# One row of the last weight matrix loaded in three unequal parts

## The chip, the cores and the metric

The kernel runs on one core of a Trainium2 chip. The metric is the device time of one execution in microseconds (us). Before the change it is 401.03 us, the median of three runs (400.92 to 401.08).

## The reference

One token (a row of 1,024 numbers, bf16) goes through two blocks side by side, and their outputs are added to it.

```python
xn = _layernorm(x)
return x + _A_ref(xn, A_k_cache, A_v_cache, A_wq, A_wo) + _B_ref(xn, B_w1, B_w2, B_w3, B_w4)

# A: attention of 32 query heads over 4 cached key/value heads of 65,536 positions, 128 wide
q = (x @ wq) as 32 heads
p = softmax(q k^T * 128 ** -0.5);  o = p v;  A = o @ wo

# B: a mixer and an MLP. For one token the shifted quarters of h are all zero,
# so the first matrix product adds nothing:
x1 = x + shifted(gelu(layernorm(x) @ w1)) @ w2
B = x1 + gelu(layernorm(x1) @ w3) @ w4
```

The weights and the caches are 170 MB, each byte of which is used once. w4 has 3,584 rows of 1,024 numbers, 7.3 MB.

## The kernel before

The kernel keeps one stream of loads going through three slots of 64 KB a partition (`big`, `SLOTS = 3`). The stream, in order, is wq, w3, w1 with w2, then for each of eight units of 32,768 keys a K tile and a V tile of 8 MB, with wo between the last K and the last V, and w4 at the end. `Stream.pump` issues the next load, on SP's queue, as soon as `done` says that a slot is free, so at most three loads are under way or in use. Every load spreads over all 128 partitions; the sixteen DMA engines take eight partitions each.

For a K tile (`compute_k`, L345) the vector engine transposes the tile in place (L357), TensorE multiplies it with the queries (L362), and the maximum, the exponential and one more transpose (L367 to L383) give the weights. For a V tile (`compute_v`, L402) TensorE multiplies the weights with the values (L412), four matmuls side by side at four places of the array, 32 columns each.

Everything that is added to the output row is gathered in one PSUM bank, `psB`. The 1,024 outputs are kept as two halves of 512: the half j lies in row 32 * j, and `row_acc(j, lhsT, rhs)` (L220) adds one product to it. TensorE writes half 0 from the array's columns from 0 on and half 1 from those from 32 on (`tile_position`), and the two matmuls of a pair can be under way together. Its callers are the start with x itself and its layer norm (L281), w2 (L340), the projection of the last head group (L449), the sum of the projections of the others (L459) and w4 (L465). In the kernel before, `row_acc` repeats the single column of weights 32 times, so that rows 0 to 31 all hold half 0 and rows 32 to 63 all hold half 1.

The end of the kernel is this. After the last K tile the slot that it held goes to w4, whose load (L179 to L184) is cut into eight pieces along the 28 rows that each partition holds: 6, 5, 6, 4, 3, 2, 1 and 1 rows (`W4_PIECES`). A row here is 1,024 numbers, 2,048 bytes, in each of the 128 partitions. The wo projections of three head groups run (L451), then the last V tile. Then come the first 11 rows of w4 (`compute_w4`, L461), the projection of the last group through `row_acc`, and the other 17 rows as their pieces land: for each row a pair of matmuls, one for each half. ScalarE casts `psB[0:64]` to bf16 (L485), and a load queue of its own stores two rows of it, 31 and 32, which lie next to each other and hold one half each (L486).

Two passes over the finished program matter here. `keep_loaded_weights` drops a weight load where the same weights stand at the same place of the array already. `close_on_the_store` makes the end of the program wait for the store alone.

Of the kernel before, what the change touches and what calls it, by code (L numbers as in the profile page):

```python
# [17 lines left out]
SUBS = 4  # L18
SETS = 4
SLOTS = 3  # L20
W4_PIECES = (6, 5, 6, 4, 3, 2, 1, 1)


def keep_loaded_weights(nc):
# [68 lines left out]
def kernel(  # L93
# [14 lines left out]
    nc = tc.nc  # L108
# [3 lines left out]
    D = A_x.shape[-1]  # L112
# [9 lines left out]
    assert DH == P and HQ // HKV == 8 and HKV == 4 and D == 1024 and F == 3584 and S == 1  # L122
    assert SK % UKEYS == 0 and sum(W4_PIECES) == FC
    NB = SK // UKEYS
# [22 lines left out]
    class Stream:  # L147
# [17 lines left out]
        def load(self, it):  # L165
            t = big.tile([P, ROW], BF16, name="big")
            self.tiles[it] = t
            go = nc.sync.dma_start
            if it == "wq":
                go(out=t[:], in_=A_wq.rearrange("(p c) n -> p (c n)", c=DC))  # L170
            elif it == "w3":
                go(out=t[:, 0:DC * F], in_=B_w3.rearrange("(p c) f -> p (c f)", c=DC))
            elif it == "w12":
                go(out=t[:, 0:DC * D], in_=B_w1.rearrange("(p c) n -> p (c n)", c=DC))
                go(out=t[:, DC * D:2 * DC * D], in_=B_w2.rearrange("(m c) n -> m (c n)", c=DC))
            elif it == "wo":
                go(out=t[:].rearrange("p (g n) -> p g n", g=HKV),
                   in_=A_wo.rearrange("(g p j) n -> p g (j n)", g=HKV, p=P))
            elif it == "w4":  # L179
                w4_v = B_w4.rearrange("(m c) n -> m c n", c=FC)  # L180
                c0 = 0
                for n in W4_PIECES:
                    go(out=t[:, c0 * D:(c0 + n) * D], in_=w4_v[:, c0:c0 + n, :].rearrange("p c n -> p (c n)"))
                    c0 += n  # L184
            else:
                kind, i = it
                g, b = divmod(i, NB)
                cache = A_k_cache if kind == "K" else A_v_cache
                go(out=t[:], in_=cache[0, g, b * UKEYS:(b + 1) * UKEYS, :].rearrange("(p ct) d -> p (ct d)", p=P))
# [8 lines left out]
    ident_f = const.tile([P, P], F32, name="ident_f")  # L198
# [9 lines left out]
    for b in range(2):  # L208
        nc.gpsimd.tensor_copy(
            out=spread[:, 2 * b:2 * b + 2, :].rearrange("p r (a i) -> p r a i", a=4),  # L210
            in_=ident_f[:, 64 * b:64 * b + 64].rearrange("p (i r) -> p r i", r=2).unsqueeze(2).to_broadcast([P, 2, 4, 32]))
# [6 lines left out]
    psB = ps_B.tile([P, 512], F32, name="psB")  # L218

    def row_acc(j, lhsT, rhs, start=False):  # L220
        nc.tensor.matmul(psB[32 * j:32 * j + 32, :], lhsT=lhsT.to_broadcast([lhsT.shape[0], 32]), rhs=rhs, start=start,  # L221
                         stop=False, tile_position=(0, 32 * j), skip_group_check=True)

    x_t = ppool.tile([P, DC, 32], BF16, name="x_t", tag="p")
    for a in range(4):
        nc.vector.transpose(out=x_t[32 * a:32 * a + 32].rearrange("p c j -> p (c j)"),  # L226
                            in_=x_row[:, 256 * a:256 * (a + 1)].rearrange("p (i c) -> p c i", c=DC))
# [3 lines left out]
    def layernorm(src, tag):  # L231
# [39 lines left out]
                          in_=sel8[:].unsqueeze(2).to_broadcast([P, 8, 16]))  # L271
# [5 lines left out]
    accx = ppool.tile([1, D], F32, name="accx", tag="p")  # L277
    nc.vector.tensor_scalar(out=accx[:], in0=x_row[0:1, :], scalar1=ln_s1[0:1, 0:1], scalar2=ln_s2[0:1, 0:1],
                            op0=ALU.mult, op1=ALU.add)
    for j in range(2):  # L280
        row_acc(j, ident_f[0:1, 0:1], accx[0:1, 512 * j:512 * (j + 1)], start=True)  # L281

    def row_matmul(acc, rep, cols, widths):
        for c in range(DC):
# [44 lines left out]
    def compute_w12():  # L329
        wt = st.tiles["w12"][:, 0:2 * DC * D].rearrange("p (w c n) -> p w c n", w=2, c=DC)  # L330
        ps1 = ps_S.tile([P, SUBS, 512], F32, name="ps1", tag="sc")
        for c in range(DC):
            for q in range(2):
                nc.tensor.matmul(ps1[0:32, q, :], lhsT=xn2_rep[:, c, :], rhs=wt[:, 0, c, 512 * q:512 * (q + 1)],  # L334
                                 start=(c == 0), stop=(c == DC - 1), tile_position=(0, 0))
        h1 = ppool.tile([32, 2, 512], BF16, name="h1", tag="p")
        nc.scalar.activation(out=h1[:], in_=ps1[0:32, 0:2, :], func=ACTF.Gelu_apprx_tanh)
        for c in range(DC):
            for j in range(2):
                row_acc(j, g_col[:], wt[:, 1, c, 512 * j:512 * (j + 1)])  # L340
        st.done("w12")
# [60 lines left out]
    def compute_v(u):  # L402
        g, b = divmod(u, NB)
        if b == 1:
            og, wb, ol = group_weights()
        vt = st.tiles[("V", u)][:].rearrange("p (s u t d) -> p s u t d", u=SUBS, s=SETS, t=16)
        oacc = ps_O.tile([P, 512], F32, name="oacc")
        pT = group["p"]
        for e in range(SUBS):
            for t in range(16):  # L410
                q = t % 4
                nc.tensor.matmul(oacc[32 * q:32 * (q + 1), :], lhsT=pT[:, e, 32 * t:32 * (t + 1)],  # L412
                                 rhs=vt[:, :, e, t, :], start=(e == 0 and t < 4),
                                 stop=(e == SUBS - 1 and t >= 12), tile_position=(0, 32 * q))
        st.done(("V", u))
        if b == 0:
            og = ogpool.tile([P, 512], F32, name="og", tag="og")
            nc.scalar.copy(out=og[:], in_=oacc[:])
            group["og"] = og
            return  # L420
        nc.vector.scalar_tensor_tensor(out=og[:], in0=oacc[:], scalar=wb[:, 1:2], in1=og[:],  # L421
                                       op0=ALU.mult, op1=ALU.add)
        group_rows(g, og, ol)
# [20 lines left out]
    def project(g):  # L444
        wt = st.tiles["wo"][:].rearrange("p (g j n) -> p g j n", g=HKV, j=8)
        for j in range(8):
            for h2 in range(2):
                if g == HKV - 1:
                    row_acc(h2, oT[g][:, j:j + 1], wt[:, g, j, 512 * h2:512 * (h2 + 1)])  # L449
                    continue  # L450
                nc.tensor.matmul(tail["rows"][0:1, h2, :], lhsT=oT[g][:, j:j + 1],  # L451
                                 rhs=wt[:, g, j, 512 * h2:512 * (h2 + 1)], start=(g == 0 and j == 0),
                                 stop=(g == HKV - 2 and j == 7), tile_position=(0, 0))
# [7 lines left out]
    def compute_w4(lo, hi):  # L461
        wt = st.tiles["w4"]
        for c in range(lo, hi):
            for j in range(2):
                row_acc(j, hT[:, c:c + 1], wt[:, D * c + 512 * j:D * c + 512 * (j + 1)])  # L465
# [9 lines left out]
    for g in range(HKV - 1):  # L475
        project(g)
    add_projection()
    compute_v(NU - 1)
    early = sum(W4_PIECES[:2])
    compute_w4(0, early)  # L480
# [3 lines left out]
    out_t = ogpool.tile([64, 512], BF16, name="out_t", tag="og")  # L484
    nc.scalar.copy(out=out_t[:], in_=psB[0:64, :])  # L485
    nc.scalar.dma_start(out=out[0, 0, :].rearrange("(j n) -> j n", j=2),  # L486
                        in_=out_t[31:33, :])

# [1 line left out]
_INS = ['A_x', 'A_k_cache', 'A_v_cache', 'A_wq', 'A_wo', 'B_x', 'B_w1', 'B_w2', 'B_w3', 'B_w4']  # L490
# [26 lines left out]
```

## Time and profile before

| what | before |
|---|---|
| median of three runs | 401.03 us |
| the profiled execution, its own time | 400.92 us |
| its span, first to last instruction | 398.9 us |
| mean granted TensorE clock | 0.803 |
| share of the span that the load queue's packets fill, of 16 engines | 98.9% |
| busy: TensorE, weight loads, VectorE, ScalarE, GpSimd | 58%, 11%, 52%, 7%, 1% |
| read from HBM | 169.87 MB, 426 GB/s |

The page gives the busy time of each engine (PE is TensorE's matmuls, PEld its weight loads, DVE VectorE, ACT ScalarE, POOL GpSimd, SP the engine that issues the loads), and the span in 40 equal slices with the busy share in tenths. Where a line of the page reads `out<-in`, it names what is written and what is read; the number after L is a line of the kernel. The chain of work that ended last is followed back from the last instruction, at each step to what released it.

Beside the pages, the trace keeps for each load the moments at which its engines reported that their part had landed, sixteen for a load on all engines, and the start, size and duration of every packet. It does not name the engine of a packet.

### The profile page before, as it was taken

To read this page: it belongs to the slowest core of one execution; us is meant where nothing else is said; L and a number is where in the kernel's file an instruction comes from. 1 tells how busy PE (TensorE), PEld (TensorE's weight loads), DVE (VectorE), ACT (ScalarE), POOL (GpSimd) and SP (SyncE) were. 2 spreads that over 40 slices of the span, in tenths; PEclk is the share of its full clock that TensorE was granted. 3 is DMA by queue.
4 is the path that set the end of the run, shared out by engine and by line. 5 is a ranking of instruction groups with operands and counts; after the bars stand their busy time and mean duration, and the time that the engine had idled before them with its cause. 6 is when DMAs were issued, how large, how long until landed. Compare 5 with 4: busy or idle time off the path is not lost.

```text
span 398.9 us, 2547 instructions
## 1 busy us (share of the span) xinstructions
PE 232.8 (58%) x1348; PEld 45.1 (11%) x854; DVE 209.0 (52%) x154; ACT 27.3 (7%) x35; POOL 5.3 (1%) x28
## 2 busy tenths in 40 slices
PE   0571970591479238742974196539462945494987
PEld 0210000010100110010101010200020101010133
DVE  0601010964196569634953895269439942884130
ACT  1001010003000200020002000200100011002000
POOL 2000000000000000000000000000000000000000
PEclk9995996596869687956795889569855997698889
DMA  9998999999999999999999999999999999999996
GB/s 421 421 454 369 440 447 486 421 427 421 416 435 421 427 493 416 427 427 427 435 421 421 486 421 427 422 427 434 434 422 460 434 427 389 424 457 447 390 418 258
DMA packets 4575, 170.01 MB, mean 426 GB/s; under 512 B 467, under 2 KB 469, under 8 KB 982
## 3 DMA queue, kind: packets, MB, share of 16 engines
q1 hardware_dynamic: 4560, 169.87, 98.9%
q8 instruction: 8, 0.13, 0.1%
q14 instruction: 1, 0.01, 0.0%
q10 hardware_dynamic: 6, 0.00, 0.0%
HBM read 169.87 MB, written 0.00 MB: 426 GB/s over the span
## 4 chain that ended last, share of the span: by engine, by line
DMA 58%; DVE 20%; PE 18%; ACT 2%; issue 1%; DVEq 0%; ACTq 0%
DMA big<-in_A_k_cache_dram 34%; DVE big L357 14%; DMA big<-in_B_w_dram 14%; DMA big<-in_A_v_cache_dram 11%; PE sc L362 7%; PE oacc L412 5%; PE psh L287 3%; DVE p_sb L383 2%; DVE mx L367 2%; ACT p_sb L380 2%; PE ps L334 1%; PE psB L221 1%; PE pm_mx L369 0%; DVE m L371 0%; DVE ol L432 0%
## 5 line engine op out<-in xcount | busy, mean ns | idle before, releaser
L362 PE MATMUL sc<-big,qdiag 128*128 128x512 bf16 x512 | 128.5, 411 | 66.3 <-DVE big L357 66.1
L357 DVE STREAM_TRANSPOSE big<-big 128x4096 f32<-128x4096 f32 x32 | 139.4, 4413 | 50.1 <-DMA big<-in_A_k_cache_dram 50.1
L412 PE MATMUL oacc<-big,p_sb 128*32 128x512 bf16 x512 | 43.9, 511 | 34.5 <-DVE p_sb L383 34.5
L367 DVE TENSOR_REDUCE mx<-sc 128x1 f32<-128x2048 f32 x8 | 18.3, 2292 | 29.8 <-PE sc L362 29.8
L362 PEld LDWEIGHTS <-qdiag 128*128 128x128 bf16 x128 | 13.1, 103 | 177.1 <-issue 145.1
L380 ACT ACTIVATE p_sb<-sc,nball 128x2048 bf16<-128x2048 f32 x8 | 15.7, 1967 | 219.8 <-DVE nball L378 219.8
L383 DVE STREAM_TRANSPOSE p_sb<-p_sb 128x2048 bf16<-128x2048 bf16 x8 | 18.5, 2311 | 18.0 <-ACT p_sb L380 18.0
L412 PEld LDWEIGHTS <-p_sb 128*32 128x32 bf16 x512 | 16.5, 124 | 58.6 <-DVE p_sb L383 35.1
L287 PE MATMUL psh<-big,ln_rep_b 128*32 128x512 bf16 (+1 forms) x64 | 12.8, 968 | 7.5 <-DMA big<-in_B_w_dram 7.5
L451 PE MATMUL o_acc<-big,oT 128*1 128x512 bf16 x48 | 13.0, 440 | 2.4 <-ACT p_sb L380 2.4
L369 PE MATMUL pm_mx<-ident_f,mx 128*1 128x128 f32 x8 | 2.4, 295 | 19.1 <-DVE mx L367 19.1
L326 DVE STREAM_TRANSPOSE h_row<-h_row 128x896 bf16<-128x896 bf16 x1 | 1.1, 1112 | 21.0 <-ACT h_row L325 21.0
L421 DVE SCALAR_TENSOR_TENSOR og<-oacc,wb,og 128x512 f32<-128x512 f32 x4 | 3.0, 746 | 15.7 <-PE oacc L412 15.7
L221 PE MATMUL psB<-big,hT 128*32 128x512 bf16 x56 | 8.3, 430 | 0.3 <-DMA big<-in_B_w_dram 0.3
L457 DVE COPY o_rows<-o_acc 1x1024 f32<-1x1024 f32 x1 | 1.2, 1212 | 13.8 <-PE oacc L412 13.8
L235 PE MATMUL pm_ln<-ln_rowsum_a,ones_f 128*128 128x1 f32 x2 | 0.6, 347 | 12.6 <-DVE ln_rowsum_a L233 12.6
L433 PE MATMUL pm_e<-ol,sel8big 128*128 128x129 f32 x8 | 2.6, 414 | 7.9 <-DVE ol L432 7.9
L287 PE MATMUL psq<-big,ln_rep_a 128*32 128x512 bf16 x64 | 6.4, 585 | 1.3 <-DMA big<-in_A_wq_dram 1.3
L311 POOL COPY qdiag<-qx 32x32 bf16<-32x32 bf16 x16 | 3.2, 203 | 279.1 <-PE sc L362 249.1
L226 DVE STREAM_TRANSPOSE x_t<-x_row 32x256 bf16<-32x256 bf16 x4 | 2.5, 616 | 8.2 <-DMA x_row<-in_A_x_dram 8.1
L299 DVE CAST q_row<-psq 128x512 bf16<-128x512 f32 x1 | 0.7, 692 | 8.4 <-PE psq L287 8.4
L376 PE MATMUL pm_mx<-ident_f,rep 1*128 1x1 f32 x8 | 1.9, 240 | 5.0 <-DVE rep L373 5.0
(95 smaller groups left out, 73.6 us busy)
## 6 DMA issues: line engine op xcount, KB each, us to landing
big<-in_A_wo_dram SPq DMA_DIRECT2D x1, 8192.0 KB, 35.9
big<-in_B_w_dram SPq DMA_DIRECT2D x1, 7168.0 KB, 38.2
big<-in_B_w_dram SPq DMA_DIRECT2D x2, 2048.0 KB, 46.0
big<-in_B_w_dram SPq DMA_DIRECT2D x2, 1536.0 KB, 27.2
big<-in_B_w_dram SPq DMA_DIRECT2D x1, 1280.0 KB, 23.9
big<-in_B_w_dram SPq DMA_DIRECT2D x1, 1024.0 KB
big<-in_B_w_dram SPq DMA_DIRECT2D x1, 768.0 KB, 30.6
big<-in_B_w_dram SPq DMA_DIRECT2D x1, 512.0 KB, 31.4
```

What stands on the lines that cost most here:

```text
L221: nc.tensor.matmul(psB[32 * j:32 * j + 32, :], lhsT=lhsT.to_broadcast([lhsT.shape[0], 32]), rhs=rhs, start=start, stop=False, tile_positio ...
L287: nc.tensor.matmul(acc[32 * q:32 * q + 32, i, 0:n], lhsT=rep[:, c, :], rhs=cols(c, i, q), start=(c == 0), stop=(c == DC - 1), tile_positio ...
L311: nc.gpsimd.tensor_copy(out=qdiag[at, LEAD:].rearrange("p (x c) -> p x c", x=4)[:, :, 32 * a:32 * a + 8], in_=qx[at, :, 8 * g:8 * g + 8])
L334: nc.tensor.matmul(ps1[0:32, q, :], lhsT=xn2_rep[:, c, :], rhs=wt[:, 0, c, 512 * q:512 * (q + 1)], start=(c == 0), stop=(c == DC - 1), til ...
L357: nc.vector.transpose(out=words, in_=words)
L362: nc.tensor.matmul(sc[:, e, :], lhsT=qdiag[:, c0:c0 + P], rhs=cols[:, s, e, :, b2, :, r], start=(s == 0 and b2 == 0 and r == 0), stop=(s = ...
L367: nc.vector.reduce_max(out=mx[:], in_=sc[:].rearrange("p e n -> p (e n)"), axis=AX.X)
L380: nc.scalar.activation(out=p_sb[:], in_=sc[:], func=ACTF.Exp, bias=nball[:, b:b + 1], scale=SCALE, accum_out=group["lall"][:, b:b + 1])
L383: nc.vector.transpose(out=flat, in_=flat)
L412: nc.tensor.matmul(oacc[32 * q:32 * (q + 1), :], lhsT=pT[:, e, 32 * t:32 * (t + 1)], rhs=vt[:, :, e, t, :], start=(e == 0 and t < 4), stop ...
L421: nc.vector.scalar_tensor_tensor(out=og[:], in0=oacc[:], scalar=wb[:, 1:2], in1=og[:], op0=ALU.mult, op1=ALU.add)
L451: nc.tensor.matmul(tail["rows"][0:1, h2, :], lhsT=oT[g][:, j:j + 1], rhs=wt[:, g, j, 512 * h2:512 * (h2 + 1)], start=(g == 0 and j == 0), ...
```

## The change

Two things change.

The piece of 4 rows of w4 becomes one of 3 rows and one of 1. That one row is loaded by three DMAs, of the first 85 partitions, the next 30 and the last 13. A DMA's partitions are shared out evenly over as many engines as divide them: 85 go to the lowest 5 engines, 17 each, 30 to the lowest 15, 2 each, and 13 to the lowest 13, 1 each. So engines 0 to 4 carry 20 partitions of this row, 5 to 12 carry 3, 13 and 14 carry 2, and 15 carries none, where each carried 8.

The repeating of the weights goes: `row_acc` loads the single column that it is given and writes one row of `psB`. Only the first call keeps 32 columns, of which 31 are zero, so that all of `psB[0:64]` is written once. The store takes rows 0 and 32.

```diff
-W4_PIECES = (6, 5, 6, 4, 3, 2, 1, 1)
+W4_PIECES = (6, 5, 6, 3, 1, 3, 2, 1, 1)
+W4_SHARED = 4
+SHARES = (85, 30, 13)
...
-                for n in W4_PIECES:
+                for i, n in enumerate(W4_PIECES):
+                    if i == W4_SHARED:
+                        p0 = 0
+                        for k in SHARES:
+                            go(out=t[p0:p0 + k, c0 * D:(c0 + n) * D],
+                               in_=w4_v[p0:p0 + k, c0:c0 + n, :].rearrange("p c n -> p (c n)"))
+                            p0 += k
+                        c0 += n
+                        continue
...
     def row_acc(j, lhsT, rhs, start=False):
-        nc.tensor.matmul(psB[32 * j:32 * j + 32, :], lhsT=lhsT.to_broadcast([lhsT.shape[0], 32]), rhs=rhs, start=start,
-                         stop=False, tile_position=(0, 32 * j), skip_group_check=True)
+        nc.tensor.matmul(psB[32 * j:32 * j + lhsT.shape[1], :], lhsT=lhsT, rhs=rhs, start=start, stop=False,
+                         tile_position=(0, 32 * j), skip_group_check=True)
...
-        row_acc(j, ident_f[0:1, 0:1], accx[0:1, 512 * j:512 * (j + 1)], start=True)
+        row_acc(j, ident_f[0:1, 0:32], accx[0:1, 512 * j:512 * (j + 1)], start=True)
...
     nc.scalar.dma_start(out=out[0, 0, :].rearrange("(j n) -> j n", j=2),
-                        in_=out_t[31:33, :])
+                        in_=out_t[:].rearrange("(a b) n -> a b n", b=32)[:, 0, :])
```

## The prediction

> **What bounds the kernel now.** I read the page first, then the chain in order of time, then the DMA share in narrow stretches at the end, then the timeline of the same stretch.
>
> ```profile
> span 398.9 us, 2547 instructions
> PE 232.8 (58%) x1348; PEld 45.1 (11%) x854; DVE 209.0 (52%) x154; ACT 27.3 (7%) x35; POOL 5.3 (1%) x28
> DMA  9998999999999999999999999999999999999996
> q1 hardware_dynamic: 4560, 169.87, 98.9%
> q8 instruction: 8, 0.13, 0.1%
> ```
>
> All sixteen DMA engines are busy from start to end (98.9% in the one load queue), and no compute engine passes 58%. The loads set the time, so only what happens when they run out can move it. The chain in order of time ends so:
>
> ```profile
> 337.13 41.98 DMA big<-in_A_v_cache_dram
> 379.11 0.02 issue
> 379.12 17.39 DMA big<-in_B_w_dram
> 396.52 0.04 issue
> 396.56 0.41 PE psB L221 x2
> 396.97 0.02 issue
> 396.99 0.58 ACT out_t L485
> ```
>
> The last piece of w4 lands at 396.52, one pair of matmuls, the cast and the store follow, and the span ends at 398.9. This execution took 400.92, 0.11 under the median of 401.03; 2.0 us of it lie around the span, and I leave them and everything after 396.52 as they are. The columns below are the stretch, its length, each engine's busy time, the clock, the DMA share and GB/s.
>
> ```profile
> 394.20:394.40 0.20, 0.20 (x6) 0.10 (x2) 0.00 (x0) 0.00 (x0) 0.00 (x0) 1.00 1.06 410
> 394.60:394.80 0.20, 0.20 (x6) 0.08 (x4) 0.00 (x0) 0.00 (x0) 0.00 (x0) 1.00 0.52 195
> 395.20:395.40 0.20, 0.20 (x4) 0.11 (x3) 0.00 (x0) 0.00 (x0) 0.00 (x0) 1.00 0.58 215
> 395.60:395.80 0.20, 0.20 (x4) 0.00 (x0) 0.00 (x0) 0.00 (x0) 0.00 (x0) 1.00 0.52 195
> 396.00:396.20 0.20, 0.20 (x2) 0.02 (x2) 0.00 (x0) 0.00 (x0) 0.00 (x0) 1.00 0.01 0
> ```
>
> The share does not fall at once: it stands between 0.5 and 0.7 for 1.4 us. Some engines have run out while about half still load. The trace's landing events of the last piece say which times: six engines report at 394.77 to 395.02, one at 395.43, one at 395.81, eight at 396.21 to 396.52. The same events tell why: after the first load only one engine stood apart (0.88 us; the others lay within 0.47), and each of the eight packets of 16 KB in the queue named instruction moves one engine back by some 1.5 us (the one at 383.06: from 0.19 to 1.73 behind the first). It stays back for good, since every load gives each engine the same eight rows. The mean of the sixteen landings is 395.75: levelling them perfectly would win 0.77 us, 0.19%. I count 0.2% (0.8 us) as what a measurement here can tell from no change, so faster by more is all but shut out.
>
> **The shared row, if rows cost what they cost now.** The price of a row (2,048 bytes into one partition) stands in the timeline, in the starts of the last two pairs:
>
> ```profile
> 395.92 0.10 PEld L221 LDWEIGHTS <-hT 128*32 128x32 bf16 x2 [0.32 <-issue]
> 396.56 0.39 PE L221 MATMUL psB<-big,hT 128*32 128x512 bf16 x2 [0.25 <-DMA big<-in_B_w_dram]
> ```
>
> They are 0.64 us apart, one piece of eight rows an engine: 0.08 us a row. In the change engines 0 to 4 take 17 + 2 + 1 = 20 rows of the shared row, 5 to 12 take 3, 13 and 14 take 2, 15 none, where each took 8. So the lowest five get 12 more (0.96 us), the rest 5 to 8 fewer (0.40 to 0.64). If those five are among the six early ones, they end at 395.73 to 395.98, and the latest of the late at 396.52 - 0.40 = 396.12: the end comes 0.40 us earlier.
>
> **What rows cost when they are crossed.** Until now an engine always wrote its own eight rows of each load. Now 20 rows of each low engine fall into partitions that other engines are filling in the same microseconds with the pieces around it. The trace shows no such meeting, so I bound it. Below: nothing, 0.08 us a row; a gain per row is excluded, since an engine alone already runs at this pace. Above: the one row where foreign bytes meet an engine's stream is the instruction packet, which put an engine back 1.54 us for 16 KB, while a 16 KB packet of its own takes 0.61 us (eight of them end 4.9 us apart, 43.04 to 47.94): 2.5 times the bytes' time, 0.20 us a row. Two streams that simply alternate lie between, 0.16. I take 0.16, for it is the nearer to the only row with a meeting, without that row's fetch delays. Then a low engine needs 20 x 0.16 = 3.20 us instead of 0.64, 2.56 more, and its last landing moves from 395.02 to 397.58, 1.06 past today's end. At 0.20 it is 3.36 more, 398.38, +1.86. The late engines, with 3 rows at 0.16 (0.48) instead of 0.64, and 8 rows of others pressed into their partitions (8 x 0.08), end at 396.52 + 0.48 = 397.00, and do not decide. The break-even price is (396.52 - 395.02 + 0.64) / 20 = 0.107 us a row, and it is slower by 0.8 us from 0.147.
>
> [...]
>
> **Issues and waits.** Eleven loads are issued for w4 instead of eight; an issue takes SP 0.33 to 0.43 us, so 1.3 us more.
>
> ```profile
> 361.56 17.89 SPq L183 DMA_DIRECT2D big<-in_B_w_dram  x8
> ```
>
> This takes 17.9 us because the eighth waits, 14.4 us, for the V load that used the same landing counter (379.11). Eight counters go round, so the eighth of the new list (three rows) waits there too, and numbers nine to eleven (2, 1 and 1 rows) wait for the first three pieces, which landed at 382.81, 385.88 and 389.58. Nothing else is queued behind them on SP but the end's own waits. The last is issued at about 389.6 + 0.4; the store's packets ran 0.75 us after its issue began, and the earliest engine reaches that piece at 394.1: 3 us of cover, cost nothing. Without it each microsecond of lateness would be one of span. The pair for the shared row waits for three loads instead of one; checks of a passed semaphore took SP 0.02 to 0.03 us. The low engines come to that row at 389.6 to 389.9 (the landings of the old four-row piece, 390.25 to 390.52, less eight rows) and end it 3.2 us later, at 393.1; PE, which is behind its loads there, comes to it at 394.29. So 1.2 us of cover; beyond that each microsecond would hold back the seven pairs behind it.
>
> **Weights of one column, and the store.** row_acc now loads one column instead of 32 copies. The loads of 32 took 97 ns (median of 56, L221), those of one column 84 (24 in the projection, L451): 13 ns each, beside matmuls that start in pairs every 0.216 us. On the path lies at most the last one: -0.01 us. Against it: L451's one-column matmuls, all in one column group, go one after another, 0.43 us for two. L221's go two at once because j = 0 and 1 stand at columns 0 and 32; those places are kept, so I count nothing (the other end is a rival). The cast still reads 64 x 512 (0.58 us). The store takes rows 0 and 32 instead of 31 and 32: two packets of 1 KB, 47 and 46 ns side by side; from nothing to 0.05 us, I take nothing.
>
> Sum: +1.06 - 0.01 on this execution (401.97), and on the median 401.03 + 1.05 = 402.1.
>
> **The rivals.** *Free crossing* (0.30): a row costs 0.08 us wherever it goes; the end is levelled, -0.40 us, 400.6. For it: the engines' pace is the same for packets of 2 and 64 KB, which reads like an engine's own limit. Against: it supposes spare room on the writing side that 98.9% busy engines never showed. This is the case on the other side; it decides below 0.107 us a row. *A late engine among the low five* (0.13): no view names the engines; if one of the eight late ones is numbered 0 to 4, its 0.96 us come on top of 396.52: 402.0 even with free crossing. For it: eight of sixteen are late. Against: the one-partition load of x fits into the stream of an engine that more likely ends early, by the packets' times, which leave two or three candidates. *Both* (0.10): 396.52 + 2.56, 403.6. *Pairs lost* (0.03): if one-column matmuls ran singly, the 25 pairs after 390.41 would take 10.8 us at 0.43 and end at 401.2, not 396.97: +4.2, 405.3. Against: the column places.
>
> **How the numbers follow.** Crossing paid, low five early: 0.40, at 402.1, own range 401.5 to 402.9, of which 0.04 lies within 0.8 us of before. Free crossing 0.30, all within it. A late engine 0.13, 0.02 of it within. Both 0.10 and pairs lost 0.03, slower. What is left, 0.04, is a gain near full levelling or beyond, faster. Slower: 0.36 + 0.11 + 0.10 + 0.03 = 0.60; same 0.36; faster 0.04. The range reaches from 400.5 (free crossing, with 0.1 for the store and spread) to 403.1 (0.20 a row, and 0.2 over), and leaves out both and pairs lost, 0.13, and half of the faster cases.
>
> **What would show it.** Crossing is right if packets of the shared row take well over 84 ns and the last landings spread wider than 1.75 us, with few engines at the very end; the DMA share would then end in a long low step. Free crossing shows as a drop from 1.0 to near 0 within 0.7 us and a last landing near 396.1. A late low engine shows as one to three landings a microsecond behind the rest, packets at 84 ns. Lost pairs show as L221 pairs 0.43 us apart with no DMA wait. The prediction is wrong above all if writing into a neighbour's partitions is free.

## The result and the profile after

The changed kernel takes 403.27 us (median of six runs, 403.03 to 403.55) against 401.10 before (six runs as well): 2.17 us more, a ratio of 1.0055 with a 95% interval of 1.0042 to 1.0068. A second set of runs of the same kernel, below, gave 403.01 against 401.14. The profiled execution took 403.40 us.

The page of the kernel after, its first lines:

```profile
span 401.3 us, 2551 instructions
PE 233.7 (58%) x1348; PEld 44.6 (11%) x854; DVE 209.0 (52%) x154; ACT 27.3 (7%) x35; POOL 5.3 (1%) x28
GB/s 418 418 446 385 457 470 431 418 418 425 420 471 438 431 425 413 438 425 470 433 418 425 425 431 438 459 431 418 425 439 425 438 451 382 425 462 438 392 391 186
q1 hardware_dynamic: 4721, 169.87, 98.7%
q8 instruction: 8, 0.13, 0.1%
```

The load queue is as full as before (98.7%), the engines' busy times are nearly the same, and the same bytes are moved. The span is 2.4 us longer, and the last slices of the GB/s row are where it went. The chain in order of time ends so:

```profile
379.49 16.24 DMA big<-in_B_w_dram
395.73 0.04 issue
395.77 3.17 PE psB L231 x14
398.94 0.02 issue
398.96 0.58 ACT out_t L495
```

The end has moved from 396.99, where the cast began, to 398.96, and the path now goes through seven pairs of matmuls instead of one: in this execution the clock granted to them was 0.50, and they stood about 0.42 us apart. The landing events put the last landing of w4 at 398.28, against 396.52; the last pair starts 0.04 us behind it in both profiles. In narrow stretches of the kernel after (columns as in the prediction: the last three are clock, DMA share, GB/s):

```profile
389.00:390.00 1.00, 1.00 (x14) 0.39 (x10) 0.09 (x1) 0.00 (x0) 0.00 (x0) 1.00 1.01 338
390.00:391.00 1.00, 1.00 (x12) 0.38 (x10) 0.00 (x0) 0.00 (x0) 0.00 (x0) 1.00 1.07 283
391.00:392.00 1.00, 1.00 (x12) 0.43 (x10) 0.00 (x0) 0.00 (x0) 0.00 (x0) 1.00 1.05 254
392.00:393.00 1.00, 0.49 (x6) 0.08 (x1) 0.00 (x0) 0.00 (x0) 0.00 (x0) 1.00 1.01 291
396.00:397.00 1.00, 1.00 (x6) 0.26 (x3) 0.00 (x0) 0.00 (x0) 0.00 (x0) 0.50 0.69 260
397.00:398.00 1.00, 1.00 (x8) 0.44 (x6) 0.00 (x0) 0.00 (x0) 0.00 (x0) 0.50 0.08 31
```

and of the kernel before, three of the same stretches:

```profile
390.00:391.00 1.00, 1.00 (x12) 0.46 (x10) 0.23 (x1) 0.00 (x0) 0.00 (x0) 1.00 1.07 446
391.00:392.00 1.00, 1.00 (x14) 0.47 (x10) 0.00 (x0) 0.00 (x0) 0.00 (x0) 1.00 0.94 387
392.00:393.00 1.00, 1.00 (x14) 0.41 (x12) 0.00 (x0) 0.00 (x0) 0.00 (x0) 1.00 1.05 428
```

This is the reading that matters most. While the shared row is loaded the DMA share stays at 1.0, but the bytes per second fall from about 420 to 254 to 338. No engine is idle; their packets take longer. A DMA share alone would have shown nothing.

The packet records say which ones. The 128 packets of the shared row took 124 ns in the mean, where packets of 2,048 bytes took 86 in the kernel before. The 256 packets of 6,144 bytes, which are the pieces of three rows before and behind it, took 299 ns where 238 was usual, and the 128 of 4,096 bytes that follow 169 instead of 162. Together that is 21.4 us more, 1.34 for each of the sixteen engines, and under a quarter of it lies in the shared row's own packets.

The store is the other place. The timeline of ScalarE at the end, after, and below it the store's issue before:

```profile
398.96 0.58 ACT L495 CAST out_t<-psB 64x512 bf16<-64x512 f32 x1 [30.75 <-PE psB L231]
399.57 0.59 ACTq L496 DMA_DIRECT2D out_dram<-out_t  x1
```

```profile
397.60 0.26 ACTq L486 DMA_DIRECT2D out_dram<-out_t  x1
```

The issue of the store takes 0.59 us, where it took 0.26. From the end of the cast to the instruction that the store's landing releases it is 1.70 us instead of 1.19.

So the 2.48 us between the two profiled spans are 1.76 for the last landing, 0.51 for the store, and 0.21 for the last pair of matmuls, from whose start to the cast it was 0.63 us instead of 0.43, at a granted clock of 0.50 to 0.52.

### The profile page after: what moved, and what is told of

Same layout as the page of the kernel before. It is cut to its first block, busy times and chain, and to the rows that moved or that the text cites. A ratio compares the mean times of both kernels' runs of the same rounds, so it can differ in the third digit from the quotient of the medians.

```text
span 401.3 us, 2551 instructions
## 1 busy us (share of the span) xinstructions
PE 233.7 (58%) x1348; PEld 44.6 (11%) x854; DVE 209.0 (52%) x154; ACT 27.3 (7%) x35; POOL 5.3 (1%) x28
## 3 DMA queue, kind: packets, MB, share of 16 engines
q1 hardware_dynamic: 4721, 169.87, 98.7%
## 4 chain that ended last, share of the span: by engine, by line
DMA 51%; DVE 26%; PE 17%; ACT 3%; another core or an unknown queue 2%; issue 1%; DVEq 0%; ACTq 0%
DMA big<-in_A_k_cache_dram 31%; DVE big L367 18%; DMA big<-in_A_v_cache_dram 10%; PE sc L372 8%; PE oacc L422 6%; DMA big<-in_A_wq_dram 5%; DMA big<-in_B_w_dram 4%; DVE p_sb L393 3%; DVE mx L377 3%; ACT p_sb L390 3%; PE psq L297 2%; PE psB L231 1%; DVE m L381 0%; PE pm_mx L379 0%
## 5 line engine op out<-in xcount | busy, mean ns | idle before, releaser
L422 PE MATMUL oacc<-big,p_sb 128*32 128x512 bf16 x512 | 45.4, 526 | 34.5 <-DVE p_sb L393 34.5
L231 PE MATMUL psB<-big,hT 128*1 128x512 bf16 x56 | 8.5, 438 | 2.1 <-DMA big<-in_B_w_dram 2.1
```

What stands on the lines that cost most here:

```text
L231: nc.tensor.matmul(psB[32 * j:32 * j + lhsT.shape[1], :], lhsT=lhsT, rhs=rhs, start=start, stop=False, tile_position=(0, 32 * j), skip_gro ...
```

## The experiments

All times are medians beside runs of the kernel before on the same chip (401.14 to 401.19), with the ratio's 95% interval. Where an edit changes only `SHARES`, it is made in the kernel of the run with the shared row alone.

**The store alone.**

```diff
-                        in_=out_t[31:33, :])
+                        in_=out_t[:].rearrange("(a b) n -> a b n", b=32)[:, 0, :])
```

> The kernel before, with one edit: the store takes rows 0 and 32 in place of 31 and 32 (all 64 rows hold the result here, so the output is the same). In the profile of the change the stretch from the end of the cast to the landing of the store grew from 1.19 to 1.70 us and the store's issue from 0.26 to 0.59. Theory 'rows 32 apart cost the store': 401.1 + 0.5 = 401.6, issue near 0.59. Rival 'it was the end of the program that ran late, or chance': 401.1, issue near 0.26.

401.68 us, +0.49, ratio 1.0014 (1.0004 to 1.0023). The timeline of its end:

```profile
397.31 0.58 ACT L485 CAST out_t<-psB 64x512 bf16<-64x512 f32 x1 [29.58 <-PE psB L221]
397.92 0.59 ACTq L486 DMA_DIRECT2D out_dram<-out_t  x1
```

The issue takes 0.59 us with nothing else changed, and the stretch from the cast to the store's landing is 1.70 us again. The choice of rows, not the late end, costs it.

**The store of two rows that are two apart.**

```diff
-                        in_=out_t[31:33, :])
+                        in_=out_t[31:35:2, :])
```

> The kernel before with rows 31 and 33 stored: two rows that hold the two halves, but not next to each other. Theory 'a store whose rows are not next to each other takes longer to issue': 401.7, issue near 0.59. [...]

401.73 us, +0.59, ratio 1.0015 (1.0006 to 1.0025):

```profile
397.82 0.69 ACTq L486 DMA_DIRECT2D out_dram<-out_t  x1
```

Rows 31 and 33 cost as much as rows 0 and 32. It is not the distance of 32; in these runs adjacent rows issue in 0.26 to 0.27 us and others in 0.59 to 0.69. Why is not shown.

**One-column weights with that store, and the old pieces.** The change with `W4_PIECES = (6, 5, 6, 4, 3, 2, 1, 1)` and no shared row.

> The change without its shared row: weights of one column, rows 0 and 32 stored, the old eight pieces of w4. Theory 'one column is free': the same as the run with the store alone, 401.6, last landing near 396.5, pairs 0.216 us apart. Rival 'one column costs or saves at the end': differs from that run by 0.2 us or more.

401.59 us, +0.40, ratio 1.0010 (1.0000 to 1.0019): what the store alone costs. The weights of one column cost and bring nothing that can be measured (0.09 us less than the run with the store alone, within both intervals).

**The shared row alone.** The diff's part in `load` and the new pieces, with the old `row_acc` and the old store.

> The shared row alone: weights of 32 columns and rows 31 and 32 stored as before, the row of w4 in 85, 30 and 13 partitions. Theory 'the shared row moves the last landing by 1.76 us, and the pair after it runs at a lower clock': 401.1 + 1.7 to 2.0 = 402.8 to 403.1, GB/s near 250 to 340 at a DMA share near 1.0 while the row is loaded. Rival 'the one-column weights had a part in it': below 402.6.

402.73 us, +1.54, ratio 1.0039 (1.0024 to 1.0054), with the last landing at 398.18 and 283 to 299 GB/s between 390 and 393 us at a DMA share of 1.00 to 1.08. It is the larger part. With the 0.40 of the run above it makes 1.94 of the 2.17; what is left is within the intervals.

**The same row, eight partitions an engine, but other partitions.**

```diff
-SHARES = (85, 30, 13)
+SHARES = (112, 16)
```

> As the run of the shared row alone, but in 112 and 16 partitions, over 16 engines both times: 7 rows and 1 row an engine, 8 in all, as before. No engine gets more or less than it had; only the partitions that it writes are others. Theory 'rows in partitions that other engines fill cost more': 0.12 to 0.16 us a row for 7 rows on every engine, 0.3 to 0.6 us later, 401.4 to 401.7, with a dip of GB/s at a full DMA share. Rival 'only the engine's own pace counts, and the loss came from a late engine that got 12 rows more': 401.1.

402.27 us, +1.08, ratio 1.0027 (1.0016 to 1.0038). No engine has more to do than before. The stretches while the row is loaded:

```profile
390.00:391.00 1.00, 1.00 (x14) 0.48 (x10) 0.00 (x0) 0.00 (x0) 0.00 (x0) 1.00 0.96 264
391.00:392.00 1.00, 1.00 (x12) 0.42 (x9) 0.00 (x0) 0.00 (x0) 0.00 (x0) 1.00 1.00 317
392.00:393.00 1.00, 0.56 (x6) 0.22 (x5) 0.00 (x0) 0.00 (x0) 0.00 (x0) 1.00 1.06 270
```

The dip is the same as in the change. The loss is about twice the upper end of what I had expected, and no engine has more rows to blame it on; what differs is which engine writes which partitions, in two loads instead of one. From the last landing of the last V tile to the last landing of w4 it is 18.48 us against 17.41 before, 1.07 us more. The packet records agree: the 128 packets of the crossed row took 113 ns in the mean instead of 86, the 256 of 6,144 bytes beside it 288 instead of 238, the 128 of 4,096 bytes 169 instead of 162. That is 17.4 us in all, 1.09 for each of the sixteen engines. Four fifths of it lie in the packets that the row meets, so a price per crossed row would miss most of the cost.

**Two such rows.** `W4_PIECES = (6, 5, 6, 2, 1, 1, 3, 2, 1, 1)`, the fifth and the sixth piece in 112 and 16 partitions, again with the old `row_acc` and the old store.

> Two rows of w4 in 112 and 16 partitions in place of one (pieces 6, 5, 6, 2, two such rows, 3, 2, 1, 1; twelve issues). Theory 'each crossed row of the load costs the same': the loss of one was 1.08 us, so 401.2 + 2.1 to 2.2 = 403.3 to 403.4. Rival 'the loss comes once, from the meeting of early and late engines, and does not grow': 402.3.

403.40 us, +2.26, ratio 1.0056 (1.0041 to 1.0071). Twice the rows, twice the loss, and the dip lasts longer:

```profile
389.00:390.00 1.00, 1.00 (x14) 0.46 (x10) 0.00 (x0) 0.00 (x0) 0.00 (x0) 1.00 0.98 254
391.00:392.00 1.00, 0.90 (x10) 0.32 (x5) 0.00 (x0) 0.00 (x0) 0.00 (x0) 1.00 0.98 268
393.00:394.00 1.00, 0.18 (x4) 0.10 (x2) 0.00 (x0) 0.00 (x0) 0.00 (x0) 1.00 1.05 240
```

**A piece in two halves of partitions.** The first piece of w4 as two loads, partitions 0 to 63 and 64 to 127, six rows each; every engine has four partitions of each.

```diff
-                    go(out=t[:, c0 * D:(c0 + n) * D], in_=w4_v[:, c0:c0 + n, :].rearrange("p c n -> p (c n)"))
+                    for p0 in ((0, 64) if c0 == 0 else (0,)):
+                        p1 = p0 + 64 if c0 == 0 else P
+                        go(out=t[p0:p1, c0 * D:(c0 + n) * D],
+                           in_=w4_v[p0:p1, c0:c0 + n, :].rearrange("p c n -> p (c n)"))
```

> The kernel before with the first piece of w4 (6 rows) loaded as two DMAs, of partitions 0 to 63 and of 64 to 127. Each engine carries the same number of rows as before, 4 and 4. Theory 'the writing side is shared by partitions': in each half two engines go into the partitions of one, so both halves take as long as the whole, the piece takes 3.7 us more, and the end comes 3 to 3.7 us later, 404.1 to 404.8, with packets of 12,288 bytes at twice their 0.46 us. Rival 'an engine's own pace is the limit': 401.1, packets at 0.46.

406.53 us, +5.35, ratio 1.0138 (1.0121 to 1.0155).

```profile
377.00:378.00 1.00, 1.00 (x7) 0.24 (x3) 0.00 (x0) 0.00 (x0) 0.00 (x0) 1.00 0.63 160
379.00:380.00 1.00, 1.00 (x6) 0.17 (x2) 0.00 (x0) 0.00 (x0) 0.00 (x0) 1.00 0.89 197
381.00:382.00 1.00, 0.82 (x16) 0.47 (x19) 0.00 (x0) 0.00 (x0) 0.00 (x0) 1.00 1.16 270
383.00:384.00 1.00, 1.00 (x26) 0.52 (x21) 0.00 (x0) 0.00 (x0) 0.00 (x0) 1.00 0.94 211
385.00:386.00 1.00, 0.00 (x0) 0.00 (x0) 1.00 (x1) 0.00 (x0) 0.00 (x0) 1.00 0.96 199
388.00:389.00 1.00, 0.82 (x6) 0.40 (x6) 0.52 (x1) 0.00 (x0) 0.00 (x0) 1.00 1.04 426
```

For ten microseconds the same sixteen engines move about half the bytes, and in the packet records a tenth of the packets of 12,288 bytes take 0.93 us or more, where before all took 0.46 to 0.47. An engine's own pace isn't the limit here. The loss is larger than the doubling of one piece (3.7 us), so I had it too small: the early engines begin on the first half while the late ones are still at the V tile, whose landings spread over 3.77 us instead of 1.8, and the bytes per second are back at 426 only from 388 us on, after 190 and 293 in the two microseconds before. The DMA share of 0.63 at the start is no mark of the halves, since the kernel before has 0.61 between 377 and 378 us; it moved 258 GB/s in that stretch, and this run 160. In the next microsecond the share is 0.52 here and 0.84 before; why is not shown. In the first five rows above the bytes come at 160 to 270 GB/s. The runs do not tell the writing from the reading side, so the theory of a shared writing side is mine and not shown.

**As many issues, no row moved.** `W4_PIECES = (6, 5, 5, 1, 1, 2, 1, 3, 2, 1, 1)`: eleven loads of all 128 partitions.

> The kernel before with w4 in eleven pieces of all 128 partitions (6, 5, 5, 1, 1, 2, 1, 3, 2, 1 and 1 rows) in place of eight: as many issues and as many waits for earlier landings as the change has, with no row moved to another engine. Theory 'issues and waits are covered': 401.1. Rival 'the later issues leave the engines dry': 401.5 or more, with a DMA share below 0.9 before the last piece.

401.47 us, +0.29, ratio 1.0008 (0.9999 to 1.0017), an interval that holds no change.

```profile
392.00:393.00 1.00, 0.95 (x8) 0.28 (x6) 0.00 (x0) 0.00 (x0) 0.00 (x0) 1.00 1.01 408
393.00:394.00 1.00, 0.03 (x2) 0.00 (x0) 0.00 (x0) 0.00 (x0) 0.00 (x0) 1.00 0.98 389
394.00:395.00 1.00, 0.45 (x6) 0.24 (x6) 0.00 (x0) 0.00 (x0) 0.00 (x0) 1.00 0.94 365
```

The engines do not run dry before the last piece, so the waits for earlier landings are covered. What is there may be the finer cutting: the first landing of the last piece comes 17.67 us after that of the V tile, against 17.47 before.

**Which engines are late.** Five small loads of k partitions, 1 KB in each, into unused room between the second and the third piece of w4:

```diff
+                    if i == 2:
+                        for q, k in enumerate((1, 2, 3, 4, 5)):
+                            go(out=t[0:k, FC * D + 512 * q:FC * D + 512 * (q + 1)], in_=w4_v[0:k, 0, 0:512])
```

> The kernel before with five small loads of 1, 2, 3, 4 and 5 partitions (1 KB each, into unused room) between the second and the third piece of w4. They go to the lowest 1, 2, 3, 4 and 5 engines, and their landing events tell engine by engine who is early and who is late. Theory 'one of the low five is late': four of the five land within 0.7 us of the first landing of the piece before, one 1.2 us or more after it. Rival 'all five are early': all within 0.7 us. Time about 401.2 by either.

401.11 us. The landing events, in us, of the second piece (sixteen engines) and of the small loads:

```
second piece  384.09 .12 .13 .21 .39 .48 .58 | 385.28 | 385.60 ... 386.07
k = 1         384.76
k = 2         384.26         384.95
k = 3         384.40 .43             385.12
k = 4         384.59 .62                     385.36 .46
k = 5         384.31 .77 .80                         385.56 .66
```

Each row has one engine more than the row above, and the others come back 0.15 to 0.25 us later. Engine 0 is early but the last of the seven early ones; engines 1, 2 and 4 are early; engine 3 is the one that lies alone, 1.2 us behind. Every trace shows how one engine comes to lie there: a single packet of 8 KB in an instruction queue, at 113.0 to 113.5 us. In this run the load that lands at 106 us has no landing between 0.50 and 1.87 us behind its first, and the next load has one at 1.18, which stays. In the kernel before it is the same (none between 0.78 and 1.83, then one at 1.15), and there this engine's last landing is the one at 395.81. That it is engine 3 in the other runs too is inferred from the packet, which comes at the same time in all of them. The count of landings, k for a load of k partitions, is also what the change's words say of 85, 30 and 13: those three loads have 5, 15 and 13 landings in its trace. No trace numbers the engines: 0 to 4 stand for the order in which the small loads add them. That a load's partitions go out evenly is inferred: four of the five landings of the first of those three loads lie at 391.80 to 392.15 us, the fifth, 1.97 behind the first of them, at 393.77.

With 6, 7, 9, 11 and 13 partitions:

> The same with small loads of 6, 7, 9, 11 and 13 partitions, which tell the engines from 5 up in ones and pairs. If the eight engines that the instruction packets hold back are the upper ones, the landings of the loads of 9, 11 and 13 add late engines; if they are spread, early and late ones are mixed. Time about 401.2.

401.46 us. The second piece landed from 384.23 on; engines 5 and 6 first appear at 386.35 and 386.15, engines 7 and 8 at 384.47 and 384.64, engines 9 to 12 at 386.1 and later. Early are 0, 1, 2, 4, 7, 8 and one of 13 to 15. The engines are mixed, not a low and a high half: the lowest five hold four early engines and one that is behind.

**Engine 3 left out.** It carries 5 partitions of the row, as most engines do, and engines 0 to 2 carry 22.

```diff
-SHARES = (85, 30, 13)
+SHARES = (51, 45, 32)
```

> The shared row alone (weights of 32 columns, rows 31 and 32 stored), in 51, 45 and 32 partitions: engines 0 to 2 carry 22 rows of it, 3 to 14 carry 5, 15 carries 2. The small loads showed engines 0, 1, 2 and 4 early and engine 3 about 1.2 us behind the first; here engine 3 gets 3 rows fewer in place of 12 more. Theory 'crossing costs everybody, engine 3 adds the last straggler': the straggler goes, the last landing 0.3 to 0.7 us earlier than with 85, 30 and 13, 402.0 to 402.5. Rival 'engine 3 was the whole loss': 400.8 to 401.2. Rival 'engine 3 has no part': 402.7 or more.

402.24 us, +1.10, ratio 1.0028 (1.0017 to 1.0038). The last landing is at 397.50 instead of 398.18, and no engine stands apart behind the others. Against 402.73 that is 0.49 less: engine 3's share was worth about half a microsecond, and the rest of the loss stays. The other engines' counts differ too in this run, so the half is not engine 3's to the last tenth.

**The changed kernel once more.**

> The changed kernel again, for two things of its profile that stand on one execution: the straggler (one engine's last landing 0.56 us behind the next) and the last seven pairs of matmuls at 0.42 us in place of 0.216, at a granted clock near 0.5. Theory 'the straggler is engine 3 and comes back': a gap of 0.4 us or more before the last landing again. For the clock no theory: if it is the throttle's chance, the pairs stand at 0.216 this time and the time is 0.2 us less in such executions. 403.2 in the median.

403.01 us, +1.87, ratio 1.0048 (1.0033 to 1.0063). The straggler is there again, 0.49 us behind the next. The clock was not:

```profile
395.91 0.81 PE L231 MATMUL psB<-big,hT 128*1 128x512 bf16 x6 [0.32 <-DMA big<-in_B_w_dram]
397.17 1.04 PE L231 MATMUL psB<-big,hT 128*1 128x512 bf16 x6 [0.45 <-DMA big<-in_B_w_dram]
398.47 0.38 PE L231 MATMUL psB<-big,hT 128*1 128x512 bf16 x2 [0.26 <-DMA big<-in_B_w_dram]
```

The pairs stand 0.216 us apart again, at a clock of 1.00. The slow pairs of the first profile came in one of two executions; the last pair took over 0.6 us also in the runs with 51, 45 and 32 partitions and with two rows, which load 32 columns. They are no mark of the one-column weights.

## Why the prediction was wrong

The direction was right: slower, at the last landings and not in a compute engine. The size was not: +1.05 was forecast, +2.17 measured, 0.17 above the top of the range. Two steps of the sum failed. It took all five low engines to be early, and engine 3 was not; and it took the store at nothing. In the profiled execution the first is worth 0.70 us (the last landing at 398.28 instead of 397.58), the second 0.51, and a low clock at the last pair, which a second execution did not have, the other 0.21. By its own steps:

*The price of a row, and the rows an engine.* Right: 0.08 us where nobody is crossed. The rival of free crossing rested on one pace for packets of 2 and of 64 KB, which is a little off: 84 ns for the one and 2,420 for the other, a tenth less by the byte.

*What rows cost when they are crossed.* Right in sign, near in amount for a loaded engine, wrong in who pays; so the nearness is luck. The sum gave a low engine 2.56 us more. Engine 3, the one that can be followed, took 2.32 more from the landing of the last V tile to its last one (378.53 to 398.28, against 378.38 to 395.81). But the sum put all of it on the 20 rows, at 0.16 us instead of 0.08. No run shows a crossed row at 0.16 us, two streams that alternate, or the fetch delays that the choice of 0.16 set aside: the packets of the shared row took 124 ns in the mean, those of 6,144 bytes beside it 299 instead of 238. Engine 3's 12 rows more make 0.96 at the usual price, and the other 1.36 is no more than the 1.34 that the packet records give an engine in the mean, whatever it carried. The late engines show it too: they were to end at 397.00 and "do not decide". In the change twelve engines, the loaded low ones and the late ones together, land between 397.07 and 397.72, and only three early ones that were not loaded land at 396.01 to 396.14. The late engines had five to eight rows fewer, and the sum gave them 0.08 for each of eight foreign rows and nothing more. How the waiting is passed on from packet to packet is not shown by these runs; that it costs every engine is.

*If those five are among the six early ones.* Failed, and with it the base of 395.02 that the 2.56 us were added to. Engine 3 was not one of the eight late ones either, which the rival "a late engine among the low five" named. It was the one between, at 395.81 in the prediction's own list, and 395.81 + 2.56 is 398.37; 398.28 was measured. The time came nearest to the rival "both", to which I gave 0.10 and 403.6 us, counted from 396.52. Leaving engine 3 out brought half a microsecond back. The hint that I used, the stream into which the load of x fits, spoke of engine 0 alone, and there it was right.

*The store.* Failed outright: "from nothing to 0.05 us, I take nothing", measured 0.5. I bounded it by the packets, 46 and 47 ns, and not by its issue, for which the trace of before held a single form. With 0.5 in the sum the forecast would have been 402.6 and the range's top 403.6.

*Weights of one column.* Right: 0.09 us between the two runs, within their intervals. Pairs are not lost: they stood 0.216 us apart in the second profiled execution of the change.

*Issues and waits.* Right, within what was measured: 0.29 us with an interval that reaches to none. The cost of cutting w4 finer, some 0.2 us by the landings, was not in my sum.

*What would show it.* Packets of the shared row well over 84 ns: yes, 124 in the mean; but those of 6,144 bytes beside it went from 238 to 299, and a tenth of them took 0.38 us or more. A spread of the last landings over 1.75 us: 2.27, with one engine at the very end. The long low step of the DMA share did not come: it was 0.69 from 396 to 397 us and 0.08 behind that, for twelve engines ended within 0.66 us. During the meeting the share stayed at 1.0, and what fell was the GB/s beside it.

## What to carry to other kernels

A load that is handed to other engines than the ones that otherwise write its partitions cost those whom it met more than itself here (four fifths of 17.4 us with 112 and 16 partitions), so one row moved off late engines delayed all sixteen: in the change the first landed at 396.01 us instead of 394.77, the last at 398.28 instead of 396.52. Read GB/s beside the DMA share: a share of 1.01 to 1.07 at 254 to 338 GB/s, where it was about 420 before, was that meeting in the change. Before work is moved off late engines, find out by small loads which engines are late, and set the most that levelling can win (here 0.77 us) against the measured loss from one moved row (1.08 us with no engine's count changed), on every engine. Price a small store on the path by its issue and landing, not by its packets: two rows that lay next to each other issued in 0.26 us here, two that didn't in 0.59 and 0.69.

## What I had not expected of the hardware

A store of two rows takes ScalarE's queue 0.26 us to issue when they are adjacent, 0.59 when they are 32 apart and 0.69 when they are two apart, and its landing comes some 0.5 us later in both of these cases. Two loads of 64 partitions in place of one of 128 cost 5.35 us where the whole piece takes 3.7. And the nine engines that lay behind were mixed: 3, 5, 6, 9 to 12 and two of 13 to 15, neither the low nor the high ones. There are nine packets that can have held them back, eight of 16 KB and the one of 8 KB. The last piece's landings spread by much the same in every run without a crossed row (1.75 to 2.07 us).
